# Attention and expert layer on one core: constant rows by DMA, held bulk loads, ordered port turns and a choice among forty orders

## The chip, the core and the metric

The kernel runs on one core of a Trainium2 chip. The core has five engines, each with its own queue of instructions that it works off in order: TensorE (PE in the profile: matrix products, into PSUM), VectorE (DVE), ScalarE (ACT), GpSimd (POOL) and SyncE (SP), which here only issues DMA transfers. Engines wait for one another by semaphores. The metric is the time of one execution on the device, in microseconds (us); smaller is better.

## The reference, cut to what matters

```python
def _attn_ref(q, k, v, s):                 # each 8 x 8 x 576 x 64, s: 8 x 8 x 576
    scores = scale * np.matmul(q, k.transpose(0, 1, 3, 2))
    causal = np.triu(np.ones((S, S), dtype=bool), k=1)
    cum = np.cumsum(np.maximum(s, 0.0), axis=-1)
    bias = -(cum[:, :, :, None] - cum[:, :, None, :])
    scores = np.where(causal, -1000000000.0, scores + np.minimum(bias, 0.0))
    attn = np.exp(scores - np.max(scores, axis=-1, keepdims=True))
    attn = attn / (np.sum(attn, axis=-1, keepdims=True) + 1e-09)
    return np.matmul(attn, v)

def _moe_ref(x, w_gate, w1, w2):           # 4608 tokens of 512, 8 experts of 1024
    flat = (x @ w_gate).flatten()
    for idx in np.argsort(-flat):          # best pair of token and expert first
        tok, e = int(idx) // E, int(idx) % E
        if assigned[tok] >= 0 or counts[e] >= cap:      # cap = 576
            continue
        assigned[tok] = e
        counts[e] += 1
    for e in range(E):
        mask = assigned == e
        out[mask] = np.maximum(x[mask] @ w1[e], 0.0) @ w2[e]
    return out
```

The attention's output, with its 64 (batch, head) planes put side by side as 4608 tokens of 512, is the x of the expert layer.

## The kernel before

**Tiling.** The 64 planes are worked in 16 groups `g` of four (two pairs `pr` of two), so the attention has 32 units, one for each pair. Queries and keys are split into a high and a low 16-bit part, so that products of 16-bit operands keep the precision. `load` (L363) brings a group's q and k into a buffer of the ring `raw` (two buffers), lets ScalarE write the high parts (L409; the first group's also L419) and VectorE the low parts (L411) into a buffer of the ring `QK` (four buffers, QK0 to QK3), and then places copies of these parts at other partitions by DMA, called moves (L416). Rows 64 to 69 of each QK buffer carry constants and, by small DMAs (L397, `auxk`), the cumulated sums. `vload` (L434) does the same for the values (loads L440 into the ring `rv`, high part L442, low part L444 into `Vl`).

**A unit.** First a score pass S (L502, and L486 for its last blocks) puts rough scores into the PSUM ring `pss` (three buffers); VectorE takes row maxima of them (L471, a reduction and a short read of its accumulator each, of 128 to 512 columns); ScalarE and GpSimd split these maxima (L518, L520, L522), TensorE turns them (L524), ScalarE copies them (L526), and a DMA writes them as rows into QK (L529, L530). Then the transposed scores T (L544, L545, L547; at the end L587 to L589) go to the ring `pst`, ScalarE exponentiates them (P, L555), GpSimd forms the rest that P's rounding left (R, L557), and TensorE multiplies P and R with the values (L618 to L620). The output is normalized (L641 to L649), turned (L681) and multiplied with the gate's weights (L692, L693). In the text S0 and T0 are the two passes of the first unit, and so on. Units 0 and 1 use QK0, units 2 and 3 use QK1.

**After the attention** come the routing, a chain of short VectorE steps, and the eight experts, which gather their tokens, turn them and do the two products (L1293, L1297, L1379).

**What sets the order.** No engine's order is written by hand. `Plan` (L88) gets every step as a task with an engine, a duration, dependences, a priority and the ring buffers that it uses, and plays a list schedule: at each point, of the tasks that could start, the one that starts first, by priority among equals. The steps are put on each engine's queue in the order in which this schedule starts them. VectorE and GpSimd share a port to the on-chip memory; tasks that use it are marked `lock`, and the schedule lets such a task start only when the other engine's is over. This is kept in the plan alone: on the chip nothing makes one wait for the other's turn. There are two plans, one for the attention and one for the routing and the experts.

**The start.** `consts` (L248) makes the constants. VectorE fills the constant rows of QK0 and of QK1 (L285, two instructions for each buffer); GpSimd issues two DMAs (L290) that copy QK1's rows to QK2 and QK3, and a gap column of each buffer is zeroed (L297 on GpSimd, L298 on VectorE). The high parts of QK1 wait for its rows and for those two DMAs (`fresh`). Ahead of S0, TensorE does 70 matmuls on zeros (L735, "warm-up"), 55 of which stand ahead of the first score matmul and 15 between score matmuls.

## Time and profile before

| | us |
|---|---|
| time of three runs | 777.54, 777.54, 775.1 (median 777.54) |
| the profiled execution | 777.66 |
| its span in the trace | 775.6 |
| attention / routing / experts in the trace, about | 16 to 310 / 310 to 363 / 363 to 776 |

The profiled execution is 777.66 - 775.6 = 2.06 longer than its span, which is the time around the program. An engine's busy time is the time in which one of its instructions ran; PEld is TensorE's loading of weights, which lies beside its products. In a timeline row, brackets give the idle time of the engine ahead of the instruction and what ended it; rows of one kind next to each other are put together (x55). "TensorE clock" is the share of full speed (2.4 GHz) that was granted: 0.50 is 1.2 GHz. In a tile's name "QK<-QK" is output and input. A DMA's issue stands on the queue of the engine that issues it (SPq, ACTq, POOLq). The rows themselves stand in a section of their own, after the change.

### The profile page before, as it was taken

The page shows a single profiled execution, that of the slowest core. Times are in us where ns is not written, and L with a number is a line of the kernel's source. Part 1 is how long each engine was busy: PE and PEld are TensorE (multiplying, and loading weights), DVE is VectorE, ACT ScalarE, POOL GpSimd, SP SyncE. Part 2 cuts the span into 40 slices and gives each one's busy share as a digit, 9 for nine tenths or more (in the row PEclk, how much of TensorE's full clock was granted, in tenths as well). Part 3 has the DMA queues.
Part 4 walks back from the last instruction along what each step waited for, and adds up shares of the span by engine and source line. Part 5 has one row for each costly group of instructions (what it writes and reads, how often), then busy time and mean ns, then how long its engine had stood idle before and what let it go on. Part 6 is the DMA issues. An engine that isn't in the chain of part 4 may idle for free.

```text
span 775.6 us, 22590 instructions
## 1 busy us (share of the span) xinstructions
PE 722.0 (93%) x8726; PEld 454.9 (59%) x8726; DVE 598.2 (77%) x2014; ACT 391.7 (50%) x794; POOL 335.3 (43%) x428
## 2 busy tenths in 40 slices
PE   9789999999999999628998999999999999999995
PEld 3457788787888888416644544545445454454542
DVE  7889999999999996678895877969788795380110
ACT  3548888888888878405334323324244232461110
POOL 7648988788878988102032041140412224202011
PEclk9679999999999999858999999999999999999998
DMA  7897768686776511106157376394845639851000
GB/s 233 195 213 202 220 175 250 172 241 196 209 203 171 156 35 64 63 35 204 42 167 200 110 113 180 129 222 133 190 156 155 187 105 262 228 180 48 15 28 34
DMA packets 89733, 118.72 MB, mean 153 GB/s; under 512 B 39246, under 2 KB 55758, under 8 KB 89614
## 3 DMA queue, kind: packets, MB, share of 16 engines
q1 hardware_dynamic: 83116, 97.82, 46.1%
q0 software_dynamic: 5952, 19.00, 8.1%
q8 instruction: 68, 1.11, 0.6%
q10 hardware_dynamic: 558, 0.47, 0.2%
q14 instruction: 39, 0.32, 0.1%
HBM read 71.67 MB, written 19.10 MB: 117 GB/s over the span
## 4 chain that ended last, share of the span: by engine, by line
PE 54%; issue 19%; DVE 13%; DMA 5%; POOL 4%; ACT 2%; SPq 1%; POOLq 0%; ACTq 0%; DVEq 0%
PE psm L1293 13%; PE psm L1379 10%; DVE pss L471 5%; PE pst L545 4%; PE pst L544 4%; PE pss L502 3%; PE po L618 3%; PE po L620 2%; PE po L619 2%; POOL out_dram L1352 2%; POOL xg L1226 2%; PE psn L1297 2%; PE po L735 2%; PE pss L681 2%; DMA xg<-xs,ids 1%
## 5 line engine op out<-in xcount | busy, mean ns | idle before, releaser
L557 POOL TENSOR_TENSOR R<-P 128x512 f16<-128x512 f32 (+1 forms) x221 | 218.9, 1016 | 26.9 <-ACT P L555 25.2
L1293 PE MATMUL psm<-xT,w1p 128*128 128x512 f16 (+1 forms) x876 | 193.1, 353 | 1.3 <-DMA xT<-xg 0.8
L1379 PE MATMUL psm<-w2p,hT 128*128 128x512 f16 x768 | 174.4, 379 | 0.0
L555 ACT ACTIVATE P<-pst 128x512 f32<-128x512 f32 (+1 forms) x224 | 119.9, 555 | 25.0 <-PE pst L547 10.3
L1297 PE MATMUL psn<-xT,w1p 128*128 128x64 f16 x768 | 129.7, 193 | 0.0
L471 DVE CUSTOM_DVE_ANT_0 pss<-pss,mS 128x512 f32<-128x512 f32 (+3 forms) x256 | 122.7, 506 | 9.0 <-PE pss L502 8.0
L1293 PEld LDWEIGHTS <-w1p 128*128 128x128 f16 x876 | 79.2, 98 | 80.0 <-issue 1.9
L1352 POOL DMA_INDIRECT out_dram<-y,ids x40 | 39.8, 995 | 198.7 <-ACT y L1390 169.6
L1379 PEld LDWEIGHTS <-hT 128*128 128x128 f16 x768 | 69.0, 98 | 80.3 <-issue 4.4
L1226 POOL DMA_INDIRECT xg<-xs,ids x40 | 43.6, 1089 | 167.3 <-DVE ids L1184 67.3
L618 PE MATMUL po<-V,P 128*128 128x65 f16 x960 | 113.8, 196 | 1.4 <-DVE xp L649 1.0
L620 PE MATMUL po<-V,R 128*128 128x65 f16 x960 | 114.0, 194 | 0.4 <-POOL R L557 0.4
L619 PE MATMUL po<-Vl,P 128*128 128x64 f16 x960 | 113.6, 193 | 0.0
L544 PE MATMUL pst<-QK 70*128 70x64 f16 (+4 forms) x512 | 108.5, 252 | 1.2 <-ACT P L555 0.7
L545 PE MATMUL pst<-QK 128*128 128x64 f16 (+4 forms) x512 | 107.8, 251 | 0.0
L619 PEld LDWEIGHTS <-P 128*128 128x128 bf16 x960 | 90.0, 100 | 9.1 <-issue 2.8
L618 PEld LDWEIGHTS <-P 128*128 128x128 bf16 x960 | 90.4, 98 | 5.9 <-issue 1.8
L1313 ACT ACTIVATE hT<-psm 128x512 f16<-128x512 f32 x64 | 38.2, 597 | 108.1 <-PE psm L1293 88.3
L620 PEld LDWEIGHTS <-R 128*128 128x128 f16 x960 | 89.9, 97 | 0.6 <-POOL R L557 0.6
L1390 ACT ACTIVATE y<-psm 128x512 f32<-128x512 f32 x32 | 19.1, 597 | 122.0 <-PE psm L1379 108.1
L502 PE MATMUL pss<-QK 67*128 67x512 f16 (+3 forms) x256 | 72.6, 307 | 4.7 <-DVE mr L471 2.4
L1297 PEld LDWEIGHTS <-w1p 128*128 128x128 f16 x768 | 67.7, 98 | 1.3
(221 smaller groups left out, 1443.4 us busy)
## 6 DMA issues: line engine op xcount, KB each, us to landing
QK<-QK SPq DMA_DIRECT2D x120, 144.0 KB
wst<-in_w_dram SPq DMA_DIRECT2D x32, 512.0 KB
wst<-in_w_dram SPq DMA_DIRECT2D x64, 256.0 KB
raw<-in_q_dram SPq DMA_DIRECT2D x32, 288.0 KB
raw<-in_k_dram SPq DMA_DIRECT2D x32, 288.0 KB
rv<-in_v_dram SPq DMA_DIRECT2D x32, 288.0 KB
xs<-xp SPq DMA_DIRECT2D x32, 256.0 KB
xs<-xp SPq DMA_DIRECT2D x8, 128.0 KB
```

What stands on the lines that cost most here:

```text
L471: return pl.add("v", dur, lambda: nc.vector.tensor_tensor_reduce(ps(), ps(), mask, 1.0, init() if init else -3e38, OP.add, OP.max, mr.t[:, ...
L502: nc.tensor.matmul(ps.t[:, :n], F()[:, q0:q0 + 128], F()[:, k0:k0 + n], start=True, stop=True)
L544: nc.tensor.matmul(ps[:, c0:c0 + n], F()[:, ks:ks + 128], F()[:, q:q + n], start=True, stop=False)
L545: nc.tensor.matmul(ps[:, c0:c0 + n], G()[:, ks:ks + 128], G()[:, q:q + n], start=False, stop=not diag)
L555: e = pl.add("a", n / 1200 + 0.171, lambda: nc.scalar.activation(P.t[:, c0:c0 + n], ps.t[:, :n], AF.Exp, scale=1.0 / YS), [x] + fresh, pri ...
L557: sub = lambda eng: eng.tensor_tensor(R.t[:, c0:c0 + n], P.t[:, c0:c0 + n], strided_hi(P.t)[:, c0:c0 + n], op=OP.subtract)
L618: nc.tensor.matmul(o[:, i], H[:, c:c + 128], V.t[:, pr, sl], start=f, stop=False)
L619: nc.tensor.matmul(o[:, i, 0:64], H[:, c:c + 128], Vl.t[:, pr, sl], start=False, stop=False)
L620: nc.tensor.matmul(o[:, i], R.t[:, c:c + 128], V.t[:, pr, sl], start=False, stop=l)
L1293: nc.tensor.matmul(ps[:, tiles[0]:tiles[-1] + 1] if len(tiles) > 1 else ps[:, tiles[0]], lhs(f, c, a), xT.t[:, tiles[0]:tiles[-1] + 1, 4 * ...
L1297: nc.tensor.matmul(pt.t[:, 64 * f:64 * f + 64], lhs(f, c, a), xT.t[:, 4, 4 * b + c, 0:64], start=s, stop=e)
L1379: nc.tensor.matmul(py.t, hT.t[:, f, a, 128 * i:128 * i + 128], w2p.t[:, f, b], start=f == 0 and k == 0, stop=f == 7 and k == 2)
```

## The change

1. **Constant rows.** VectorE makes a template `rowc` of 320 columns (two instructions) once. QK0's rows are still filled by VectorE; those of QK1, QK2 and QK3 are written by two DMAs each from the template, issued by GpSimd, QK1's early.
2. **Bulk loads held.** The raw loads of group 2 and the value loads of groups 0 and 1 wait for the first moves (`self.first`: the copies of the high parts) of groups 0 and 1. The high parts of groups 1 and up no longer wait for the constant rows (the passes still do). Moves of group 1 may go on ScalarE's queue too. The router's constants come after QK1's.
3. **Turns at the port.** In the attention's plan each `lock` step of VectorE or GpSimd gets a real dependence on the last such step of the other engine, so that on the chip the turns are taken as in the plan. The plan counts 0.06 for handing over. The experts' plan has no `tc`, and gets none.
4. **Choice of order.** `run` draws 40 orders (all task durations varied by up to 3%; order 0 is without that), replays each four times in its fixed order with random lengthening, and emits the one in which TensorE ends earliest on the mean. A few planned durations change (TensorE's by 1.016, and hops between engines).

```diff
@@ class Plan
+    HAND = 0.06
+    tc = None
+    AFTER = {("t", "a"): 0.05, ("a", "p"): 0.05, ("v", "t"): 0.01}
...
+    ORDERS, SPREAD, DRAWS, NOISE = 40, 0.03, 4, 0.03
+
+    def run(self):
...
+        best = None
+        for n in range(self.ORDERS):
+            reset(n)
+            order = []
+            if not self.order(order.append):
+                continue
+            took = sum(self.replay(order, random.Random(d), clean[0]) for d in range(self.DRAWS)) / self.DRAWS
+            if best is None or took < best[0]:
+                best = took, n
+        reset(best[1])
+        self.order(lambda z: self.emit(*z))
+
+    def replay(self, order, draw, free):
...
+            more = x.occ / x.w * draw.uniform(0.0, self.NOISE)
...
+            if x.lock and e in "vp":
+                t = max(t, port["p" if e == "v" else "v"])
+                port[e] = t + occ + self.HAND
...
+        return max(x.begun for x in self.tasks if x.left == "t")
...
-            return dur, dur + 0.19
+            return dur * 1.016, dur * 1.016 + 0.19
...
+    def emit(self, x, f, e, *_):
+
+        made = f()
+        if x.lock and e in "vp" and self.tc:
+            other = self.held["p" if e == "v" else "v"]
+            if other is not None:
+                self.tc.add_manual_dep(made.ins, other.ins.name, mybir.DependencyInfo(
+                    mybir.DependencyClass.Sync, mybir.DependencyReason.SCHED_ONLY), reason="port")
+            self.held[e] = made
@@ class Attention
+        self.pl.tc = tc
...
+        self.rowc = self.c.tile([128, 2, 320], F16, name="rowc")
+        k["rowc"] = [pl.add("v", 0.2, lambda c=c: nc.vector.tensor_scalar(
+            self.rowc[64:70, c], self.mZ.bitcast(F16)[64:70, 0:320], self.vec[64:70, c:c + 1], None, op0=OP.add),
+            [k["vec", 0, 4], k["vec", 1, 1], k["mZ"]], prio=-93, lock=True) for c in (1, 0)]
...
-            if i < 2:
+            if i < 1:
...
-                made.append(pl.add("p", 0.9, lambda rows=rows: nc.gpsimd.dma_start(rows, self.r["QK"].slots[1][0][64:70, 0]),
-                                   self.rows1 + [k["QK", 1]], prio=-20, kb=62))
-                self.moved.append(made[0])
+                for c in (1, 0):
+                    made.append(pl.add("p", 0.9, lambda rows=rows, c=c: nc.gpsimd.dma_start(
+                        rows[:, c].rearrange("p r (n c) -> p (r n) c", c=320),
+                        self.rowc[64:70, c:c + 1, :].to_broadcast([6, 8, 320])), k["rowc"],
+                        prio=-92 if i == 1 else -20, kb=31))
...
-                          alt=("a", 0.62, lambda: f(nc.scalar.dma_start)) if both and g == 0 else None, **kw)
+                          alt=("a", 0.62, lambda: f(nc.scalar.dma_start)) if both and g < 2 else None, **kw)
...
-                ld[r, t] = Sy(0.5, lambda d, r=r, t=t: d(raw.t[:, t, r], srcs[t][b, :, 2 * hf + r]),
+                ld[r, t] = Sy(0.5, lambda d, r=r, t=t: d(raw.t[:, t, r], srcs[t][b, :, 2 * hf + r]), self.first if g == 2 else [],
...
-        if g == 1:
-            fresh = fresh + self.moved
-
...
-                         [ld[r, t] for r in range(a, z)] + fresh[:1], prio=t0 - 5 + off + t / 10, uses=[raw, QK]) for t in range(2)]
+                         [ld[r, t] for r in range(a, z)] + (fresh[:1] if g == 0 else []), prio=t0 - 5 + off + t / 10,
+                         uses=[raw, QK]) for t in range(2)]
...
+            if a == 0 and g < 2:
+                self.first = e1 + [q2, k2]
...
-        ld = [pl.add("s", 0.45, lambda r=r: nc.sync.dma_start(rv.t[:, r], self.vN[b, :, 2 * hf + r]), prio=t0 - 4.5, uses=[rv],
-                     kb=295, bulk=True) for r in range(2)]
+        ld = [pl.add("s", 0.45, lambda r=r: nc.sync.dma_start(rv.t[:, r], self.vN[b, :, 2 * hf + r]), self.first if g < 2 else [],
+                     prio=t0 - 4.5, uses=[rv], kb=295, bulk=True) for r in range(2)]
...
-        x = None
+        x = self.k["QK", 1]
```

The diff adds lines, so the same step has another number behind it (L285 is L385, L411 is L509, L444 is L544, L471 is L571, L502 is L602).

What the change moves on the engines is seen in three places. The first is SyncE's queue at the start. Before, ahead of QK1's first moves (L416 on QK_92, the last row here; each waits for a high part) stand the loads of group 2 (raw0), of the values (rv) and of the gate's weights (wgf):

```order
L382 DMA raw_87<-in_q_dram 128x576
L416 DMA QK_91<-QK_91 64x576
L382 DMA raw_87<-in_q_dram 128x576
L416 DMA QK_91<-QK_91 64x576
L382 DMA raw_87<-in_k_dram 128x576 x2
L440 DMA rv_90<-in_v_dram 128x576
L327 DMA wgf<-in_w_gate_dram 128x4x8
L440 DMA rv_89<-in_v_dram 128x576
L416 DMA QK_92<-QK_92 64x2x576 x4
```

After (moves L514, raw loads L482, value loads L540, sums L494):

```order
L514 DMA QK_92<-QK_92 64x2x576 x2
L494 DMA QK_92<-auxk 3x2x576 x2
L514 DMA QK_92<-QK_92 64x2x576
L494 DMA QK_93<-auxk 3x2x576
L514 DMA QK_91<-QK_91 64x576
L540 DMA rv_89<-in_v_dram 128x576
L494 DMA QK_93<-auxk 3x2x576
L494 DMA QK_94<-auxk 3x2x576 x2
L482 DMA raw_87<-in_q_dram 128x576 x2
L514 DMA QK_92<-QK_92 64x2x576
L482 DMA raw_87<-in_k_dram 128x576 x2
L540 DMA rv_90<-in_v_dram 128x576 x2
```

QK1's first moves stand ahead of the loads of group 2, three of them on this queue and the fourth on ScalarE's; the k loads of that group (raw0<-in_k_dram) stand behind a QK1 move that waits for VectorE's low parts. Before, those k loads waited for no VectorE step.

The second place is the end of S1 on VectorE and on TensorE. VectorE before, with the value's low part (L444) and then QK1's (L411) between row maxima of the second unit (mr_106; QK_92 is QK1):

```order
L444 SCALAR_TENSOR_TENSOR Vl_98<-rv_89,V_95 128x1152
L471 ISA pss_124,mr_106<-pss_124,mS 128x512
L471 ISA mr_106 128x1
L411 SCALAR_TENSOR_TENSOR QK_92<-raw_88,QK_92 128x2x576 x2
L471 ISA pss_122,mr_106<-pss_122,mS 128x256
```

After:

```order
L509 SCALAR_TENSOR_TENSOR QK_92<-raw_88,QK_92 128x2x576 x2
L571 ISA pss_124,mr_106<-pss_124,mS 128x512
L571 ISA mr_106 128x1
L571 ISA pss_122,mr_106<-pss_122,mS 128x256
L571 ISA mr_106 128x1
L544 SCALAR_TENSOR_TENSOR Vl_98<-rv_89,V_95 128x1152
```

QK1's low parts (L509) went ahead of the maximum over 512 columns, and the value's low part (L544) behind two more maxima. TensorE at the same place, before: the last matmul of S1 (L486) and the start of T0 (L544, L545):

```order
L486 MATMUL pss_124<-QK_91 128x512
L544 LDWEIGHTS QK_91
L544 MATMUL pst_126<-QK_91 128x512
L545 LDWEIGHTS QK_91
L545 MATMUL pst_126<-QK_91 128x512
```

After:

```order
L586 MATMUL pss_124<-QK_91 128x512
L602 LDWEIGHTS QK_92
L602 MATMUL pss_122<-QK_92 128x128
L644 LDWEIGHTS QK_91
L644 MATMUL pst_126<-QK_91 128x512
L645 LDWEIGHTS QK_91
```

The first matmul of the score pass on QK1 (L602 from QK_92) went ahead of T0's first (L644). Ahead of S0's first matmul stand 61 warm-up matmuls in place of 55, and 9 in place of 15 between the score matmuls.

The third place is a turn at the port, some units later, on VectorE (names with their buffer numbers, and what each row waits for). Before:

```order
L471 ISA pss1_123,mr2_107<-pss1_123,mZ_131,mr2_107 128x512 [waits DVE_49,PE_49]
L471 ISA mr2_107 128x1
L444 SCALAR_TENSOR_TENSOR Vl2_100<-rv1_90,V2_97 128x1152 [waits DMAHW1_49,DMAHW0_49]
L645 TENSOR_TENSOR po0_128<-po0_128,den0_114 128x5x64 [waits DVE_49]
L471 ISA pss0_122,mr0_105<-pss0_122,mS_130 128x128 [waits PE_49]
```

After:

```order
L571 ISA pss2_124,mr0_105<-pss2_124,mZ_131,mr0_105 128x512 [waits DVE_49,PE_49]
L571 ISA mr0_105 128x1
L544 SCALAR_TENSOR_TENSOR Vl2_100<-rv1_90,V2_97 128x1152 [waits DMAHW5_49,DMAHW4_49,Pool_49]
L509 SCALAR_TENSOR_TENSOR QK3_94<-raw1_88,QK3_94 128x2x576 [waits DMAHW6_49,DMAHW2_49,DMAHW1_49]
L509 SCALAR_TENSOR_TENSOR QK3_94<-raw1_88,QK3_94 128x2x576 [waits DMAHW7_49,DMAHW5_49,DMAHW1_49]
```

The low part (L544) now waits for GpSimd too (Pool), as the maxima behind it then do by standing behind it. In the attention 15 of the 46 low parts of whole groups (7 of L509, 8 of L544) got such a wait, and some 20 GpSimd steps (11 of R, 9 of the split of the maxima) got one for VectorE; before, no low part waited for GpSimd.

## Rows read from the trace of the kernel before

**Rows 1.** Windows: length, busy us (instructions) of each engine, TensorE clock, DMA share, GB/s.

```profile
16.00:310.00 294.00, 283.48 (x5200) 227.35 (x5198) 277.44 (x912) 234.94 (x540) 231.36 (x261) 0.97 0.66 182
...
363.00:776.00 413.00, 396.60 (x3043) 202.03 (x3039) 269.24 (x917) 133.23 (x215) 81.38 (x115) 0.99 0.50 138
```

**Rows 2.** Windows by the granted clock at the start; columns as above.

```profile
16.00:26.70 10.70, 7.39 (x40) 3.21 (x38) 10.25 (x37) 3.96 (x6) 2.48 (x4) 1.00 0.87 243
26.70:47.20 20.50, 17.63 (x142) 11.80 (x141) 16.95 (x48) 10.42 (x19) 12.66 (x16) 0.50 0.89 191
47.20:57.30 10.10, 8.48 (x135) 5.88 (x133) 8.89 (x30) 5.68 (x15) 5.28 (x10) 1.00 0.96 208
```

**Rows 3.** Windows of the steady attention; columns as above.

```profile
57.30:234.50 177.20, 174.48 (x3353) 143.00 (x3352) 174.10 (x571) 153.08 (x351) 146.28 (x160) 1.00 0.73 208
234.50:293.80 59.30, 59.30 (x1170) 49.03 (x1168) 57.75 (x205) 48.12 (x118) 50.69 (x57) 1.00 0.41 114
```

**Rows 4.** Timeline, TensorE: start, us, line, tiles, shape, count [idle before <-releaser].

```profile
1.61 14.34 PE L735 MATMUL po<-mZ 128*128 128x512 f16 x55 [1.61 <-DVE mZ L258]
...
26.73 0.59 PE L544 MATMUL pst<-QK 70*128 70x512 f16 x1
...
36.08 0.50 PE L502 MATMUL pss<-QK 67*128 67x128 f16 x2 [1.04 <-DMA QK<-auxk]
```

**Rows 5.** Timeline, VectorE; columns as above.

```profile
16.16 0.30 DVE L471 CUSTOM_DVE_ANT_0 pss<-pss,mS 128x128 f32<-128x128 f32 x1 [2.67 <-PE pss L502]
...
21.70 0.88 DVE L285 TENSOR_SCALAR QK<-mZ,vec 6x2560 f16<-6x2560 f16 x1
...
24.23 1.35 DVE L444 SCALAR_TENSOR_TENSOR Vl<-rv,V 128x1152 f16<-128x1152 f32 x1
25.50 0.69 DVE L471 CUSTOM_DVE_ANT_0 pss<-pss,mS 128x512 f32<-128x512 f32 x1
...
26.11 2.62 DVE L411 SCALAR_TENSOR_TENSOR QK<-raw,QK 128x1152 f16<-128x1152 f32 x2
28.65 0.42 DVE L471 CUSTOM_DVE_ANT_0 pss<-pss,mS 128x256 f32<-128x256 f32 x1
...
31.57 0.92 DVE L331 SCALAR_TENSOR_TENSOR wgp<-wgf,wgp 128x32 f16<-128x32 f32 x1
...
36.38 0.30 DVE L471 CUSTOM_DVE_ANT_0 pss<-pss,mS 128x128 f32<-128x128 f32 x1 [2.56 <-PE pss L502]
```

**Rows 6.** Timeline, GpSimd.

```profile
21.46 0.21 POOL L522 TENSOR_TENSOR mp<-ms,mp 128x10 f16<-128x10 f32 x1 [6.14 <-ACT ms L520]
...
23.90 1.32 POOL L290 DMA_DIRECT2D QK<-QK  x2 [0.31 <-POOL QK L297]
```

**Rows 7.** Timeline, ScalarE.

```profile
18.42 1.17 ACT L442 ACTIVATE V<-rv 128x1152 f16<-128x1152 f32 x1 [6.92 <-DMA rv<-in_v_dram]
...
23.40 2.22 ACT L409 ACTIVATE QK<-raw 128x1152 f16<-128x1152 f32 x2 [0.78 <-ACT mt L526]
```

**Rows 8.** Chain that ended last, first 60 us: start, us, what.

```profile
24.37 1.22 DVE Vl L444
...
26.72 6.87 DMA QK<-QK
33.60 2.46 DMA QK<-auxk
```

**Rows 9.** Timeline, SyncE's DMA queue.

```profile
21.27 0.83 SPq L382 DMA_DIRECT2D raw<-in_k_dram  x2
```

**Rows 10.** By form, 16 to 310: count | busy, mean ns | idle before <-releasers.

```profile
L557 POOL TENSOR_TENSOR R<-P 128x512 f16<-128x512 f32 x187 | 202.9, 1108 | 24.9 <-ACT P L555 23.2 <-PE po L693 1.2
...
L411 DVE SCALAR_TENSOR_TENSOR QK<-raw,QK 128x1152 f16<-128x1152 f32 x30 | 42.1, 1410 | 0.0
...
L444 DVE SCALAR_TENSOR_TENSOR Vl<-rv,V 128x1152 f16<-128x1152 f32 x16 | 23.7, 1479 | 0.0
```

**Rows 11.** Waits of TensorE, 363 to 776: total us, times, longest.

```profile
PE psm L1241 <- DMA xg<-xs,ids: 3.7, 3, 1.7
```

82 lines of the change are left out of this document (69 added, 13 removed).

## The prediction

> **What bounds the kernel now.** I read the stages first [rows 1]. In the attention stretch (16 to 310) TensorE is busy 283.48 of 294.00 and VectorE 277.44: both are nearly full, so removing work from one alone gives little there. The routing stretch (310 to 363) is a chain of short VectorE steps; in the experts TensorE is busy 396.60 of 413.00 at a granted clock of 0.99.
>
> Next I cut the attention by clock [rows 2]. From 16 to 26.7 TensorE works only 7.39 of 10.70 while VectorE works 10.25: VectorE's row maxima of the first two score passes (I call a score pass S0, S1, ..., and the transposed scores that follow T0, T1, ...) set the pace. At 26.7 the clock falls to half and stays there for 20.50 us; TensorE is busy 17.63 of them, at double price. From 47.2 to 57.3 the clock is full, and 1.62 (10.10 - 8.48) are idle. After that [rows 3] the two engines run almost without a gap: 174.48 and 174.10 of 177.20. The same kinds of matmul go through at 3353/177.20 = 18.92 per us from 57.3 to 234.5, but at 1170/59.30 = 19.73 from 234.5 to 293.8, where bulk loads are over (DMA share 0.41 against 0.73). At the later pace the long stretch would take 3353/19.73 = 169.9, so the room in it is 7.3 us. That is all that a better order of the steady part could bring.
>
> At the start [rows 4, 5]: 55 warm-up matmuls take 14.34; T0's first matmul starts at 26.73, and the first score pass on the second buffer (QK1) at 36.08, after 1.04 of idle for the DMA that brings its constant and bias rows. VectorE waits 2.67 for the first scores (16.16) and 2.56 for those of QK1 (36.38).
>
> **Constant rows.** Two VectorE fills are gone for QK1: one of 0.88 at 21.70, in the middle of S1's maxima, and one that fell into the idle ahead of 16.16 [rows 5]. The template costs two much shorter VectorE instructions ahead of S0, where VectorE has 2.67 idle: nothing. Instead GpSimd issues six DMAs. An issue like it took 1.32/2 = 0.66 and GpSimd idles 6.14 ahead of 21.46 [rows 6], so six take 3.96 of that, and the transfers are 31 KB each. Covered: 0. A gain of their own they cannot bring, for that is counted at the fill; if the cover were gone, 3.96 would stand ahead of S1's split and of T0.
>
> **The early order.** The high parts of QK1 (ScalarE) no longer wait for the fill. Before, they ran at 23.40 for 2.22, though ScalarE stood idle for 6.92 up to 18.42 [rows 7]. Now they and the first two moves of QK1 can go in that idle, by about 18. A move took 6.87 and the bias rows after it 2.46 [rows 8], so the data of the next score pass are there at about 27.5 instead of 36.08.
>
> T0 itself gets later. There are 61 warm-up matmuls ahead of S0 instead of 55; at 14.34/55 = 0.26 each that is +1.6 [rows 4]. VectorE's chain from the first maximum (16.16) to the point at 24.37 where L444 really begins, without the fill's 0.88, is 7.33. Then, by the new order, come the two low parts of QK1 (2.62), the 512-column maximum (0.69) and the 256-column one (0.42), while L444 falls behind [rows 5, 8]: 16.16 + 1.6 + 7.33 + 2.62 + 0.69 + 0.42 = 28.8. Only then have TensorE's last S1 matmuls and the first of the new pass a free PSUM buffer, and T0 stands behind them. So T0 starts at 28.8, 2.1 late, but the pass on QK1 starts there as well, 7.3 earlier than 36.08.
>
> What comes of it at 57.3, by two ledgers. *TensorE's:* before, half-clock work done by 47.2 was (20.50 - 2.87)/2 = 8.8 us of full-clock work [rows 2]. Now there are 18.4 us from 28.8 to 47.2; the 1.04 wait is gone, the other 1.83 may stay or go: (18.4 - 1.83)/2 = 8.3 to 18.4/2 = 9.2. That is -0.5 to +0.4, taken as 0. From 47.2 to 57.3 I take two thirds of the 1.62 idle as removed, as VectorE then runs ahead: +1.0. *VectorE's:* saved are the fill 0.88, the wait of 2.56, and the 0.92 step at 31.57 that now stands in the idle ahead of S0 [rows 5]; lost is the later start, 1.6: net 2.8. The gain is between 1.0 and 2.8; I take **2.0**, a little nearer the middle than to TensorE's. Ends: -1.5 (the clock comes back 2.1 later too, which costs half of that, and the -0.5) to +2.8.
>
> **Held loads.** The raw loads of the third group and the value loads of the first two now stand behind the first moves. DMA is busy 0.87 to 0.96 of the time up to 57.3 [rows 2], so this shares the same capacity out in another order. One thing is lost: two k loads of the third group, issued at 21.27 [rows 9], now stand on SyncE's queue behind a QK1 move that waits for VectorE's low parts, which end at about 27.7. They come 6.4 late. What is queued behind them is two value loads and more moves; who waits is ScalarE's high part of QK2. I give it 0, since the row maxima of S1 and of QK1's two passes cover it, and keep up to +3 (half of 6.4) for the no-change rival.
>
> **Turns at the port.** In the attention each VectorE or GpSimd instruction that uses the shared port waits for the last such instruction of the other engine in the plan. Behind such a wait on VectorE stand row maxima, for which TensorE waits. What could be gained: the 46 low parts (L411, L444) took 42.1 + 23.7 = 65.8 [rows 10], against 46 x 1.35 = 62.1 at the duration of an undisturbed one [rows 5]: 3.7 stretched by GpSimd. By the order with its waits, 15 of the 46 wait for GpSimd; their stretch turns into a wait of the same length, and the other 31 lose theirs: 31/46 x 3.7 = 2.5. The choice among forty drawn orders has no row of its own; whatever it brings lies within the same 7.3. I take **2.5**, near the stretch that the rows show rather than the whole room, between -5.2 (the last rival) and +7.3.
>
> **The experts.** Their plan has no port waits and is only one of forty near-equal orders; TensorE's queue hardly differs. The largest wait there that an order could touch is 3.7 in 3 times, 1.7 the longest [rows 11]. I take 0, plus or minus 1.7.
>
> **Sum:** 2.0 + 2.5 + 0 = 4.5. The profiled execution took 777.66 (span 775.6), 0.12 above the median 777.54, so it may stand for it: 777.66 - 4.5 = **773.2**.
>
> **Rivals.**
> *The clock.* The half-clock stretch begins when TensorE has waited through S1, and lasts 20.50 us although TensorE is busy 17.63 of them [rows 2]. The new order closes the 1.04 wait and puts score and transposed work side by side; the clock might come back after a quarter of the stretch or not fall at all. The whole stretch costs 17.63/2 = 8.8, half of it 4.4; the middle, 6.6, gives 766.6. Against it: up to 28.8 TensorE waits as much as before or more. The Trainium skill (TensorE: Matmul & The Clock Gate, "What's actually happening") says that the throttled state is the default and that activity releases it; by that rule closer work would bring the clock back sooner, and these rows, 20.50 us at half with TensorE 86% busy, do not bear it out well.
>
> *It does not do what it says.* The pass on QK1 comes 7 us earlier, but VectorE still has to do the same maxima, and the k loads of the third group come later; the early gain is spent by 57.3, and the steady part, with both engines at 98%, goes on at 18.92 per us. That gives 777.7, or with the 3 of the late loads 780 at most.
>
> *The row DMAs are held by VectorE.* If each of the six issues must wait for one VectorE instruction like the low parts (2.62/2 = 1.31), they take 6 x (0.66 + 1.31) = 11.8, which is 5.7 more than the idle 6.14: 773.2 + 5.7 = 778.9. Against it: the two issues from 23.90 ran beside L444 in 1.32 [rows 5, 6]. The Trainium skill (SBUF — State Buffer, "SBUF: two separate sides") warns of this: a DMA issued by GpSimd needs descriptors that GpSimd cannot write while VectorE holds the shared port. It speaks against this change; the row just named does not show it.
>
> *Slower: waits for a turn.* A fixed order makes VectorE wait for GpSimd's residual (L557, 1.108 mean [rows 10]) even when GpSimd is late, where before the first to come went first. If the 15 low parts that wait for GpSimd each stand half of one, 0.55, VectorE loses 8.3. Its slack from 57.3 to 234.5 is 177.20 - 174.10 = 3.1 [rows 3], so 5.2 reach TensorE: 777.66 - 2.0 + 5.2 = 780.9. It decides from a mean wait of (3.1 + 2.0)/15 = 0.34 on (no gain left); at 0.50 it is slower by 0.3%. For it: VectorE has no other room. Against: GpSimd is idle 24.9 in L557's rows alone, most of it waiting for ScalarE [rows 10], so it is seldom late by a whole instruction.
>
> **How the numbers follow.** About 0.3%, 2.3 us, is what a measurement of this kernel can tell from no change: faster is below 775.2, slower above 779.9. Forecast (769 to 775.2) 0.45; clock back early 0.10; nothing changed 0.21; row DMAs held 0.04; waits for a turn 0.20. Faster 0.45 + 0.10 = 0.55, same 0.21 + 0.04 = 0.25, slower 0.20. The range reaches from 765.5 (the clock rival less 1.1 for the uncertain steady part) to 781.5 (the slower rival and 0.6); left out are half of the slower rival's spread and a little of the clock's, under 2 in 10.
>
> **What would show it.** Right: no 0.88 fill ahead of T0, T0 at about 28.8, the first score matmul of QK1 at about 28.5 instead of 36.08; a half-clock stretch of about 20 us; L411's and L444's means near 1.36; some 19.2 matmuls per us in the long stretch. Wrong: row DMAs of over 1.5 each; VectorE idle for GpSimd's L557 (over 5 us in all); TensorE waiting for QK2's moves between 40 and 57; an experts stretch that changes by more than 2 us.

## The result, and the profile after

The changed kernel takes 785.41 us (median of 4, 783.52 to 786.9) against 777.54 for the kernel before, 7.87 more. The ratio on record is 1.0123, with a 95% interval of 1.01 to 1.0145; the quotient of the two medians is 1.0101, which lies inside it. It is **slower by 1.0 to 1.2%**, where 773.2 was forecast and 781.5 was the upper end. The profiled execution, the slowest of the four, took 786.9, with a span of 785.2 (before 775.6).

To see where it went, both traces are cut where TensorE has done the same number of matmuls (warm-ups left out). The table gives the time at which a mark is reached.

| mark | before | after | difference |
|---|---|---|---|
| first score matmul (S0) | 15.79 | 22.07 | +6.3 |
| first transposed score (T0) | 26.73 | 35.87 | +9.1 |
| start of the long stretch of 4427 matmuls | 67.7 | 70.0 | +2.3 |
| its end | 296.4 | 304.7 | +8.3 |
| first product of the experts (L1293, then L1394) | 361.0 | 370.2 | +9.2 |
| end of the span | 775.6 | 785.2 | +9.6 |

So 8.3 of the 9.6 are lost ahead of the routing and 0.9 between there and the experts, which take about as long as before. Two things stand out: a start that is 6 to 9 us late, and a stretch of the same number of matmuls that takes 6 us longer. In between, TensorE catches up much of the first.

The start. Windows of the changed kernel by the granted clock (columns as in [rows 2], which answer to it):

```profile
16.00:21.20 5.20, 1.87 (x9) 0.67 (x7) 1.47 (x4) 1.26 (x2) 1.25 (x5) 1.00 0.39 43
21.20:28.00 6.80, 5.93 (x19) 2.56 (x20) 4.09 (x17) 2.22 (x2) 4.12 (x14) 0.50 0.84 211
28.00:31.70 3.70, 2.20 (x13) 1.01 (x12) 3.21 (x17) 0.58 (x3) 0.79 (x3) 0.96 0.53 135
31.70:51.90 20.20, 17.43 (x161) 12.19 (x161) 15.55 (x46) 9.29 (x18) 6.95 (x10) 0.50 0.70 201
51.90:60.00 8.10, 7.97 (x94) 5.37 (x92) 7.63 (x29) 7.24 (x16) 6.28 (x8) 1.00 0.71 190
```

There are two half-clock stretches, 6.80 and 20.20 long, where before had one of 20.50. GpSimd's timeline at the start, then VectorE's, then TensorE's, then three pieces of the chain that ended last:

```profile
3.14 0.12 POOL L370 MEMSET vec<- 32x1 f32 x2 [2.61 <-DVE V L354]
...
6.21 0.53 POOL L357 TENSOR_SCALAR_AFFINE_SELECT mU<-mU 64x64 bf16<-64x64 bf16 x2
11.92 3.66 POOL L391 DMA_DIRECT2D QK<-rowc  x6 [5.18 <-DVE rowc L376]
```

```profile
6.78 0.88 DVE L385 TENSOR_SCALAR QK<-mZ,vec 6x2560 f16<-6x2560 f16 x1 [3.69 <-POOL mU L357]
...
8.17 0.88 DVE L385 TENSOR_SCALAR QK<-mZ,vec 6x2560 f16<-6x2560 f16 x1
9.07 1.35 DVE L450 TENSOR_TENSOR_SCAN xp<-xp,mZ 64x576 f32<-64x576 f32 x1
...
22.48 0.43 DVE L571 CUSTOM_DVE_ANT_0 pss<-pss,mS 128x256 f32<-128x256 f32 x1 [3.24 <-PE pss L602]
...
31.62 2.62 DVE L509 SCALAR_TENSOR_TENSOR QK<-raw,QK 128x1152 f16<-128x1152 f32 x2
```

```profile
1.62 16.26 PE L835 MATMUL po<-mZ 128*128 128x512 f16 x61 [1.62 <-DVE mZ L354]
22.07 0.80 PE L602 MATMUL pss<-QK 67*128 67x256 f16 x3 [4.20 <-issue]
...
34.96 1.01 PE L586 MATMUL pss<-QK 67*128 67x512 f16 x2 [2.56 <-DVE mr L571]
35.77 0.31 PE L602 MATMUL pss<-QK 67*128 67x128 f16 x1
35.87 0.63 PE L644 MATMUL pst<-QK 70*128 70x512 f16 x1
```

```profile
13.64 0.45 DVE QK L509
14.09 6.88 DMA QK<-xp
20.97 1.10 issue
```

GpSimd's first constant waits 2.61 for VectorE's memsets (3.14), and VectorE's first fill of QK0's rows then waits 3.69 for GpSimd's masks (6.78): turns at the port among the constants, where a fill reads nothing of the masks that it waits for. The scan that starts the cumulated sums runs at 9.07; before it ran at 5.50. The sums' row for S0 leaves at 14.09, takes 6.88 and lets S0 start at 22.07, after 4.20 of idle (the row says "issue", the chain shows the transfer). Then L385 is gone from S1 and the low parts of QK1 stand at 31.62, as the order said; T0 follows S1's end at 35.87, and QK1's pass starts at 35.77, no earlier than before [rows 4].

The long stretch, before and then after (windows; both have about 4427 matmuls, though not quite the same ones: after has 0.3% more columns, by estimate 0.8 us of the 6.0):

```profile
67.70:296.40 228.70, 226.26 (x4428) 186.68 (x4425) 223.60 (x748) 194.34 (x454) 190.85 (x210) 1.00 0.64 181
```

```profile
70.00:304.70 234.70, 230.91 (x4427) 188.25 (x4425) 224.35 (x744) 194.25 (x455) 170.14 (x209) 1.00 0.65 183
```

VectorE is as busy as before (223.60 and 224.35) but the stretch is 6.0 longer. After's rows by form that answer to [rows 10], over this stretch, and VectorE's waits in it (total, times, longest), before and after:

```profile
L657 POOL TENSOR_TENSOR R<-P 128x512 f16<-128x512 f32 x156 | 157.8, 1040 | 25.3 <-ACT P L655 15.5 <-DVE Vl L544 5.0 <-DVE QK L509 4.7
...
L509 DVE SCALAR_TENSOR_TENSOR QK<-raw,QK 128x1152 f16<-128x1152 f32 x26 | 34.2, 1351 | 0.0
...
L544 DVE SCALAR_TENSOR_TENSOR Vl<-rv,V 128x1152 f16<-128x1152 f32 x14 | 18.9, 1353 | 0.1
```

```profile
DVE pss L471 <- PE pss L502: 1.3, 5, 0.5
```

```profile
DVE pss L571 <- PE pss L602: 3.2, 10, 0.5
DVE pss L571 <- PE pss L586: 1.3, 6, 0.3
```

The low parts run at 1.35 and the residuals at 1.04: the stretching by the port is gone altogether, as intended. In return VectorE waits more often for scores (the listed waits 1.3 before, 3.2 + 1.3 after), and GpSimd waits for VectorE's low parts (5.0 + 4.7).

### The profile page after: what moved, and what is told of

The parts are those of the page before. It is cut to its first block, busy times and chain, and to the rows that moved or that the text cites. A ratio compares the mean times of both kernels' runs of the same rounds, so it can differ in the third digit from the quotient of the medians.

```text
span 785.2 us, 22607 instructions
## 1 busy us (share of the span) xinstructions
PE 730.8 (93%) x8726; PEld 458.1 (58%) x8726; DVE 590.5 (75%) x2018; ACT 389.8 (50%) x793; POOL 311.4 (40%) x429
## 4 chain that ended last, share of the span: by engine, by line
PE 55%; issue 19%; DVE 15%; POOL 6%; DMA 3%; ACT 1%; POOLq 0%; SPq 0%; DVEq 0%; ACTq 0%
PE psm L1394 12%; PE psm L1480 11%; DVE pss L571 4%; PE pst L644 4%; PE pst L645 4%; PE pss L602 3%; PE po L718 3%; PE po L720 2%; PE po L719 2%; POOL out_dram L1453 2%; POOL R L657 2%; DVE QK L509 2%; PE psn L1398 2%; PE pss L781 2%; PE pss L586 2%
## 5 line engine op out<-in xcount | busy, mean ns | idle before, releaser
L657 POOL TENSOR_TENSOR R<-P 128x512 f16<-128x512 f32 (+1 forms) x223 | 204.1, 948 | 38.9 <-ACT P L655 22.5
L1394 PE MATMUL psm<-xT,w1p 128*128 128x512 f16 (+1 forms) x876 | 194.0, 353 | 1.2 <-ACT xT L1344 1.1
L571 DVE CUSTOM_DVE_ANT_0 pss<-pss,mS 128x512 f32<-128x512 f32 (+3 forms) x256 | 123.3, 505 | 12.5 <-PE pss L602 11.0
L1453 POOL DMA_INDIRECT out_dram<-y,ids x40 | 41.5, 1038 | 218.6 <-ACT y L1491 189.3
L655 ACT ACTIVATE P<-pst 128x512 f32<-128x512 f32 (+1 forms) x224 | 118.0, 554 | 20.5 <-PE pst L647 9.3
L1394 PEld LDWEIGHTS <-w1p 128*128 128x128 f16 x876 | 79.4, 98 | 80.6 <-issue 2.6
L644 PE MATMUL pst<-QK 70*128 70x64 f16 (+4 forms) x512 | 105.9, 250 | 0.1
L645 PE MATMUL pst<-QK 128*128 128x64 f16 (+4 forms) x512 | 105.4, 250 | 0.0
L602 PE MATMUL pss<-QK 67*128 67x512 f16 (+3 forms) x256 | 74.4, 313 | 6.8 <-issue 4.2
L1416 DVE SCALAR_TENSOR_TENSOR hT<-psm,hT 128x512 f16<-128x512 f32 x64 | 43.9, 686 | 39.5 <-ACT hT L1414 37.9
```

The costliest lines, as they stand in the source:

```text
L571: return pl.add("v", dur, lambda: nc.vector.tensor_tensor_reduce(ps(), ps(), mask, 1.0, init() if init else -3e38, OP.add, OP.max, mr.t[:, ...
L602: nc.tensor.matmul(ps.t[:, :n], F()[:, q0:q0 + 128], F()[:, k0:k0 + n], start=True, stop=True)
L644: nc.tensor.matmul(ps[:, c0:c0 + n], F()[:, ks:ks + 128], F()[:, q:q + n], start=True, stop=False)
L645: nc.tensor.matmul(ps[:, c0:c0 + n], G()[:, ks:ks + 128], G()[:, q:q + n], start=False, stop=not diag)
L655: e = pl.add("a", n / 1200 + 0.171, lambda: nc.scalar.activation(P.t[:, c0:c0 + n], ps.t[:, :n], AF.Exp, scale=1.0 / YS), [x] + fresh, pri ...
L657: sub = lambda eng: eng.tensor_tensor(R.t[:, c0:c0 + n], P.t[:, c0:c0 + n], strided_hi(P.t)[:, c0:c0 + n], op=OP.subtract)
```

## The experiments

Each group of runs has its own runs of the kernel before, so the ratio is what counts (as on record; the quotient of the medians differs from it by up to 0.3%). "Stretch" is the time that the long stretch takes in one trace (before 228.7, after 234.7). Runs are numbered by group; the expectations say "call" for a group.

| run | rows by DMA | held loads | waits for turns | hand-over | orders | ratio to before (95%) | stretch |
|---|---|---|---|---|---|---|---|
| changed kernel | yes | yes | all | 0.06 | 40 | 1.0123 (1.0100 to 1.0145) | 234.7 |
| 1.1 | yes | yes | none | 0.06 | 40 | 1.0153 (1.0096 to 1.0210) | 246.1 |
| 1.2 | yes | yes | all | 0 | 40 | 1.0126 (1.0077 to 1.0175) | 237.6 |
| 1.3 | yes | yes | after constants | 0.06 | 40 | 1.0038 (1.0010 to 1.0065) | 235.8 |
| 1.4 | yes | yes | all | 0.06 | 1 | 1.0114 (1.0080 to 1.0147) | 233.0 |
| 2.1 | yes | yes | none | 0 | 1 | 1.0105 (1.0085 to 1.0124) | 238.1 |
| 2.2 | yes | yes | after constants | 0 | 1 | 1.0108 (1.0084 to 1.0133) | 241.4 |
| 2.3 | no | no | after constants | 0 | 1 | 1.0038 (1.0019 to 1.0057) | 232.4 |
| 2.4 | yes | yes | none | 0 | 40 | 1.0061 (1.0038 to 1.0083) | 240.5 |
| 3.1 | no | no | none | 0 | 1 | 0.9985 (0.9958 to 1.0013) | 228.7 |
| 3.2 | yes | yes | after constants | 0.06 | 40 | 0.9992 (0.9977 to 1.0007) | 234.7 |
| 3.3 | yes | yes | after constants | 0.06 | 40 | 1.0064 (1.0043 to 1.0086) | 233.3 |
| 3.4 | no | yes | after constants | 0.06 | 40 | 1.0015 (1.0002 to 1.0027) | 232.5 |
| 4.1 | yes | no | none | 0 | 1 | 1.0135 (1.0108 to 1.0163) | 240.1 |
| 4.2 | no | yes | none | 0 | 1 | 1.0068 (1.0050 to 1.0085) | 239.7 |
| 4.3 | no | no | after constants | 0.06 | 1 | 1.0045 (1.0024 to 1.0066) | 237.2 |
| 4.4 | no | yes | after constants | 0.06 | 40 | 0.9979 (0.9965 to 0.9993) | 232.6 |
| 5.1 | yes | yes | constants only | 0.06 | 40 | 1.0227 (1.0202 to 1.0251) | 246.9 |
| 5.2 | no | no | all | 0 | 1 | 1.0153 (1.0123 to 1.0182) | 232.8 |

The columns tell of the attention's plan. The experts are planned by forty orders in all of them, with the numbers of before (no hand-over, no 1.016, no extra hops) in 2.1 to 2.4, 3.1, 3.2, 4.1 to 4.4 and 5.2 (in 4.3 with the hand-over), with the changed ones elsewhere (in 1.2 the hand-over is 0 there too). This shows in the ratios: from the first product of the experts to the end the traces take 414.6 before, 412.8 to 415.7 with the changed numbers, and 409.4 to 412.6 in all eleven runs with those of before. So the ratios of these eleven hold some 2 to 5 us that aren't the attention's. Runs 3.3 and 3.4 are described below.

**Group 1: which part of the change.** Run 1.1 takes the added waits out and leaves the order:

```diff
-        self.pl.tc = tc
```

> The changed kernel, same instruction order on every engine, without the added waits between VectorE and GpSimd. Theory O (the order that the plan made costs the time: low parts stand three in a row on VectorE, 4.05 us; the waits cost only at the start): first score matmul at about 17.9 instead of 22.07, first transposed score at about 30 instead of 35.87, from 70 to 300 us the same pace as the changed kernel (about 6 us slower than before), L657 stretched again; time 783 (781 to 784.5). Rival W (the waits cost the time): the whole loss goes, time 777 (775 to 779).

Run 1.2 sets the hand-over in the plan to 0:

```diff
-    HAND = 0.06
+    HAND = 0.0
```

> The changed kernel with the hand-over of 0.06 in the plan set to 0 and nothing else; waits between the engines stay. All 46 low parts then stand alone on VectorE. Theory O: the pace from 70 to 300 us is that of before again, so 6 us of the loss go; the start still has waits among the constants; time 779.5 (777 to 782). Rival W: more changes of turn and so more waits, 785 or more.

Run 1.3 keeps the waits, but not for the steps of the constants (with which the sums, the gate's weights and the router's constants count here):

```diff
-            if other is not None:
+            if other is not None and x.rank >= self.steady:
...
         self.k["router"] = x
+        pl.steady = pl.n
```

> The changed kernel, same order, with the added waits only for steps after the constants. Theory O: the steady waits cost nothing that shows, so this is within 1.5 us of the run without any waits: 783 (781 to 785), first score matmul at about 17.9. Rival W: the steady waits cost 6, so 783 here against 777 there.

Run 1.4 takes the first drawing:

```diff
         self.pl.tc = tc
+        self.pl.ORDERS = 1
```

> The changed kernel with the attention's order taken from the first, undisturbed drawing instead of the best of forty. Theory O: the bunches of three are there as well (11 of them against 10), so the time is that of the changed kernel within 2 us: 785 (783 to 787). Rival: the replay chooses an order that is bad on the chip, and the first drawing gives 780 or less.

Measured: 789.36, 786.58, 778.61 and 785.18, where before gave 775.25. On 1.1 and 1.3 both theories fell; 1.2 came as W had it (785 or more) and 1.4 as O had it. Without any waits the kernel is not better but, if anything, worse (1.0153); with the waits after the constants alone it loses only 0.4%. So the waits are two things: those after the constants are worth about 9 us *in this order* (1.1 against 1.3, whose intervals leave 4 to 14), and those among the constants cost about 7 (1.3 against the changed kernel). VectorE and then TensorE at the start of 1.3:

```profile
3.12 0.92 DVE L385 TENSOR_SCALAR QK<-mZ,vec 6x2560 f16<-6x2560 f16 x1
...
4.65 1.00 DVE L385 TENSOR_SCALAR QK<-mZ,vec 6x2560 f16<-6x2560 f16 x1
5.69 1.35 DVE L450 TENSOR_TENSOR_SCAN xp<-xp,mZ 64x576 f32<-64x576 f32 x1
```

```profile
1.62 15.74 PE L836 MATMUL po<-mZ 128*128 128x512 f16 x61 [1.62 <-DVE mZ L354]
18.71 0.51 PE L602 MATMUL pss<-QK 67*128 67x256 f16 x3 [1.35 <-issue]
...
30.06 0.63 PE L644 MATMUL pst<-QK 70*128 70x512 f16 x1
```

The fills stand at 3.12 and 4.65 instead of 6.78 and 8.17, S0 at 18.71 instead of 22.07, T0 at 30.06 instead of 35.87. The clock goes with it: in 1.3 it stands at 0.50 for 6.80 us ahead of the long stretch, where the changed kernel has 6.80 and 20.20 and the kernel before 20.50:

```profile
27.00:33.80 6.80, 4.65 (x25) 2.64 (x25) 5.42 (x13) 2.87 (x4) 1.86 (x2) 0.50 0.93 221
```

One trace could be chance, but every execution has its mean granted clock on record. As these traces show only the two levels 0.50 and 1.00, 2 x (1 - clock) x span is an estimate of an execution's time at half clock. On the mean that is 64 us in the changed kernel (clock 0.9592, four executions), 52 in 1.3 (0.9662, ten) and 60 in the kernel before (0.9614, 79). In the long stretch, the windows of 1.1 and of 1.3, and 1.1's rows by form:

```profile
61.30:307.40 246.10, 234.58 (x4428) 189.40 (x4425) 234.78 (x745) 195.38 (x455) 207.04 (x210) 1.00 0.62 175
```

```profile
60.70:296.50 235.80, 231.21 (x4428) 188.34 (x4425) 224.49 (x745) 194.22 (x455) 170.44 (x209) 1.00 0.65 182
```

```profile
L656 POOL TENSOR_TENSOR R<-P 128x512 f16<-128x512 f32 x157 | 179.0, 1165 | 15.3 <-ACT P L654 13.7 <-ACT den L740 0.8 <-PE po L719 0.2
...
L508 DVE SCALAR_TENSOR_TENSOR QK<-raw,QK 128x1152 f16<-128x1152 f32 x26 | 38.9, 1530 | 0.0
...
L543 DVE SCALAR_TENSOR_TENSOR Vl<-rv,V 128x1152 f16<-128x1152 f32 x14 | 22.2, 1586 | 0.0
```

Without the waits this order sets VectorE and GpSimd against each other: low parts of 1.53 and 1.59, residuals of 1.17, and 246.1 for the stretch. With them 235.8. Neither comes to 228.7.

The hand-over (1.2) was expected to give 6 us back, as the low parts then stand singly (46 alone; with it, 10 triples). It gave nothing: VectorE then waits for GpSimd's residuals, which in the changed kernel's long stretch it hardly did:

```profile
DVE QK L509 <- POOL R L657: 3.2, 12, 0.4
DVE Vl L544 <- POOL R L657: 2.7, 8, 0.6
```

The choice among forty (1.4) changes nothing that can be told apart (785.18 against 785.41).

**Group 2: the parts without the new plan numbers.** Run 2.1 is the first two parts alone; 2.2 adds the waits after the constants, 2.3 puts these waits on the kernel before's own order, 2.4 is 2.1 with forty orders. 2.1's edit of the changed kernel:

```diff
-    HAND = 0.06
+    HAND = 0.0
...
-    AFTER = {("t", "a"): 0.05, ("a", "p"): 0.05, ("v", "t"): 0.01}
+    AFTER = {}
...
-            return dur * 1.016, dur * 1.016 + 0.19
+            return dur, dur + 0.19
...
-        self.pl.tc = tc
+        self.pl.ORDERS = 1
```

> Parts 1 and 2 of the change alone (constant rows by DMA, held loads) in the attention: no added waits, hand-over 0, the planned durations of before, one order instead of forty. Theory P (the first two parts gain 6 to 8 us at the start; the steady loss of 6 to 7 belongs to the turns and to the plan's numbers): a lead of about 6 at 65 us that is kept, time 770 (767 to 773). Rival Q (the lead cannot be kept in any order, since both engines are full): 776 (774 to 779).

2.2 (and 2.3, which has the kernel before's `consts`, `load` and `vload` as well) adds to that the lines of 1.3 and:

```diff
+        self.pl.tc = tc
```

> As the first run of this call, with the added waits for all steps after the constants. Without the hand-over in the plan the low parts stand alone and VectorE changes turn with GpSimd often. Theory P: VectorE waits some 7 us for L657, and the kernel is 5 us slower than the run without waits: 775 (772 to 778). Rival R (keeping the planned turns is worth about 10 in any order, as it was in the changed kernel's order): 5 or more faster than the run without.

> The attention of the kernel before, instruction for instruction, with the added waits for all steps after the constants and nothing else. Theory P: the waits replace a stretch of 3.7 by waits of 5 to 8 on VectorE: 779 (777 to 782), against 775 of before here. Rival R: 770 or less.

2.4 leaves out `self.pl.ORDERS = 1`.

> As the first run of this call, but the best of forty orders by the replay. Theory P: no difference beyond 2 us to the run with one order, since the replay does not know what stretches on the chip: 770 (767 to 774). Rival: the replay picks an order that is better by 4 or more, 766 or less.

Measured: 782.08, 782.49, 776.22 and 778.71; before 773.42. The lead at the start is there in 2.4 (5.3 us at 67.7, with T0 at 28.71, where 28.8 was forecast for the changed kernel) and small in 2.1 (1.7, T0 at 33.84), but both lose 9 to 12 in the long stretch. Waits on the order of before (2.3) cost 3.8 there, of the expected kind. Its window and VectorE's waits:

```profile
66.30:298.80 232.50, 229.77 (x4428) 188.22 (x4424) 221.91 (x748) 196.49 (x454) 172.09 (x211) 1.00 0.63 178
```

```profile
DVE QK L508 <- POOL R L655: 3.6, 14, 0.5
DVE Vl L542 <- POOL R L655: 1.2, 5, 0.3
```

VectorE now waits 3.6 + 1.2 for residuals. So of theory P, the waits' cost holds for before's order (2.3 against 3.1, which has the same attention without waits: 1.0038 and 0.9985). It isn't seen in the whole time of 2.2 against 2.1 (1.0108 and 1.0105), where P had 5 us and rival R as much the other way. That the first two parts gain 6 to 8, and keep it, fell, and so did rival Q's 776. Forty orders gave 3.4 (2.1 against 2.4), a little more than expected.

**Group 3: the experts, and what delays S0.** 3.1 has before's attention and only the experts planned anew; 3.2 is 1.3 with the experts planned by the numbers of before:

```diff
-    HAND = 0.06
+    HAND = 0.0
...
-    AFTER = {("t", "a"): 0.05, ("a", "p"): 0.05, ("v", "t"): 0.01}
+    MUL = 1.0
+    AFTER = {}
...
-            return dur * 1.016, dur * 1.016 + 0.19
+            return dur * self.MUL, dur * self.MUL + 0.19
...
         self.pl.tc = tc
+        self.pl.HAND, self.pl.MUL = 0.06, 1.016
+        self.pl.AFTER = {("t", "a"): 0.05, ("a", "p"): 0.05, ("v", "t"): 0.01}
```

> The attention of the kernel before, instruction for instruction, and of the change only the choice among forty orders for the routing and the experts, planned with the numbers of before (no hand-over, no factor 1.016, no extra hops). Theory E (in the runs with these numbers the experts ended 3.5 to 5.6 us earlier against the attention than before, while with the changed numbers they gained 0 to 1.4): time 4 less than before, 770 (768 to 772) where before gives 774. Rival: the gain came from what the attention left over at its end, and the time is that of before.

> The changed kernel with the added waits only after the constants (the third run of the first call, same attention order), and the routing and experts planned with the numbers of before. Theory E: 3 to 4 us less than that run, so about 1 us below before: 773 (771 to 776). Rival: no change against that run, 777.

3.3 is 1.3 with the gate's weights loaded later; 3.4 is 1.3 with `consts` filling the rows as before:

```diff
-        ld = pl.add("s", 0.35, lambda: nc.sync.dma_start(self.wgf, self.wg.rearrange("(c p) e -> p c e", p=128)), prio=-1,
+        ld = pl.add("s", 0.35, lambda: nc.sync.dma_start(self.wgf, self.wg.rearrange("(c p) e -> p c e", p=128)), [self.k["auxk"]], prio=-1,
```

> As the third run of the first call, but the load of the gate's weights (16 KB in many small packets, there issued at 5.61 ahead of the sums' rows) waits for the sums' last transfer. Theory F (that load holds up the small DMAs of the sums' rows, of which one took 6.90): first score matmul right behind the 59 warm-ups, at about 17.5 instead of 18.71, rows under 4 us. Rival G (the six row DMAs of GpSimd hold them up): first score matmul at 18.7 or later. The steady order is drawn anew, so the whole time is open within 6 us: 777 (772 to 784).

> As the third run of the first call, but with the constant rows made as before (two VectorE fills for QK1, two copies for QK2 and QK3). Theory F: the sums' rows are as late as there, the first score matmul at 18.7 or later (63 warm-ups, 18.3 at the earliest). Rival G: it follows the warm-ups at 18.3, and the rows land in under 4 us. The fills cost VectorE 0.88 in the second unit. Whole time open within 6 us: 778 (772 to 784).

Measured: 774.33, 776.18, 781.88 and 777.65; before 776.51. The experts' gain in the traces (2.7 us in 3.1, 3.7 in 3.2, from the first product to the end) shows as 0.9985 and, against 1.3, 0.9992 after 1.0038; neither can be told from the kernel before. On S0: moving the load of the gate's weights (3.3) left 1.69 and 0.66 of idle ahead of the first two groups of scores (the first ends with a high part of ScalarE, the second with a row of the sums), while with the old rows (3.4) S0 follows the warm-ups at once, though the load of the weights is early there too (5.5). So theory G held and F fell:

```profile
1.61 16.06 PE L832 MATMUL po<-mZ 128*128 128x512 f16 x63 [1.61 <-DVE mZ L354]
17.51 0.49 PE L598 MATMUL pss<-QK 67*128 67x256 f16 x3
```

**Group 4: rows, holds, bunches, and a better version.** 4.1 is 2.1 with before's `load` and `vload`, 4.2 is 2.1 with before's rows; no line is new. 4.3 is 2.3 with the hand-over:

```diff
-    HAND = 0.0
+    HAND = 0.06
```

> Attention with part 1 alone (constant rows by DMA from the template), no added waits, the numbers of before, one order; experts as in the last two calls. Theory G (the six row DMAs hold up the sums' rows): over 1.3 us of idle between the warm-ups and the first score matmul, as in the run with parts 1 and 2. Theory S (without waits every newly drawn order loses in the steady part, since it sets low parts and residuals against each other): from the same point of TensorE's work at about 68 to that at about 296 it takes 234 to 241 instead of 228.6; time 781 (777 to 785). Rival: only one of the two parts disturbs the steady order, and this one gives 774 to 777.

> Attention with part 2 alone (loads held behind the first moves, the high parts of the second group not waiting for the constant rows), otherwise as the run above. Theory G: no idle between the warm-ups and the first score matmul. Theory S: the steady part takes 234 to 241; time 780 (776 to 784). Rival: 772 to 775, if the loss of both parts together is that of the rows.

> Attention of the kernel before with the hand-over of 0.06 in the plan and the added waits after the constants; neither the rows nor the holds nor forty orders. The low parts then stand in bunches, as in the changed kernel. Theory B (a bunch of three makes VectorE wait for scores afterwards): VectorE waits 5 or more us for score matmuls in the steady part instead of 2.0, which takes 233 to 236 instead of 228.6. Rival (the bunches are harmless, the rows and holds disturb the order): 229 to 231.

4.4 joins 3.4 with the lines of 3.2.

> The version to which the runs point: held loads, waits only after the constants, forty orders, constant rows as before, and the experts planned with the numbers of before. Its attention is that of the fourth run of the last call, 0.5 us ahead of before at its end; the experts bring 3 to 4: 773 (771 to 775) where before gives 776.5. Rival: the experts' gain isn't there in the whole time, 776 to 777.5.

Measured: 784.28, 778.97, 775.85 and 771.63; before 773.84. TensorE at the start of 4.1 and of 4.2:

```profile
1.61 14.42 PE L834 MATMUL po<-mZ 128*128 128x512 f16 x57 [1.61 <-DVE mZ L354]
19.15 0.92 PE L601 MATMUL pss<-QK 67*128 67x128 f16 x3 [3.12 <-DMA auxk<-xp]
```

```profile
1.61 13.22 PE L831 MATMUL po<-mZ 128*128 128x512 f16 x53 [1.61 <-DVE mZ L354]
14.66 0.49 PE L598 MATMUL pss<-QK 67*128 67x256 f16 x3
```

4.1 idles 3.12 ahead of S0, 4.2 not at all. Over all runs this is clean: each run with row DMAs by GpSimd has between 1.32 and 6.93 of idle there, and each without has none, but for 5.2, where the constants wait for turns. (Between 52 and 68 warm-ups stand ahead of S0, so the size of this idle can't be compared.) SyncE's queue shows where the time goes. Run 2.1 differs from 4.2 by the way the rows are made alone, and first 2.1, then 4.2 have:

```profile
11.54 3.95 SPq L427 DMA_DIRECT2D wgf<-in_w_gate_dram  x1
```

```profile
11.55 0.65 SPq L423 DMA_DIRECT2D wgf<-in_w_gate_dram  x1
```

In both the same rows of the sums and `auxk` stand next on this queue, so in 2.1 they are 3.3 us later, and S0 starts at 18.52 instead of 14.66. In the long stretch both parts lose alike (240.1 and 239.7): it is not one of them alone that disturbs the order; each new order that was run without waits behind the constants (1.1 and 5.1, which share one, 2.1, 2.4, 4.1, 4.2) takes 238 to 247. Bunches (4.3): the stretch and VectorE's waits for scores:

```profile
61.50:298.80 237.30, 230.06 (x4427) 187.25 (x4425) 227.26 (x743) 193.45 (x455) 171.10 (x209) 1.00 0.66 179
```

```profile
DVE pss L569 <- PE pss L600: 3.7, 11, 0.6
DVE pss L569 <- PE pss L584: 1.3, 7, 0.3
```

The expected 5 us of waits for scores are there (3.7 + 1.3), and the stretch is 237.2, above the forecast.

4.4 takes 771.63 against 773.84, 0.9979 (0.9965 to 0.9993): it beats both kernels, the one before by 0.2%, half of what was expected. In its trace, 5.9 us shorter than before's, 4.5 of these lie in the experts (410.1 against 414.6), so this is no proof of a gain in the attention.

**Group 5: the waits among the constants alone.** 5.1 is 1.3 with the condition turned round, 5.2 is 2.3 with all waits.

```diff
-            if other is not None and x.rank >= self.steady:
+            if other is not None and x.rank < self.steady:
```

> The changed kernel, same order, with the added waits only among the constants and none after them: the fourth corner beside the changed kernel (both), the run without any waits, and the one with the waits after the constants. Theory C (the waits among the constants cost 6 to 8 by a first score matmul 3 to 4 us later and a half-clock stretch more, whatever the rest does): first score matmul at about 22, time 7 above the run without waits, 1.024 of before, that is about 794 (790 to 798). Rival: the loss at the start is given back in the steady part, and the time is that of the run without waits, 1.015 of before.

> Attention of the kernel before with all added waits, among the constants too; against the run of before's attention with the waits after the constants only (1.0038 of before). Theory C: the first score matmul comes 3 to 7 us later than its 16, and the time is 1.010 to 1.013 of before: 782 to 784. Rival: with before's order of the constants the waits cost nothing, 1.004.

Measured: 793.4 (1.0227) and 787.94 (1.0153); before 775.82. TensorE at the start of 5.1:

```profile
1.61 15.19 PE L836 MATMUL po<-mZ 128*128 128x512 f16 x61 [1.61 <-DVE mZ L354]
21.99 0.80 PE L602 MATMUL pss<-QK 67*128 67x256 f16 x3 [5.19 <-DMA QK<-xp]
```

With 1.1, 1.3 and the changed kernel, this is a square in one and the same order: no waits 1.0153, among the constants 1.0227, after them 1.0038, both 1.0123. The waits among the constants cost 0.74% (5.7 us) alone and 0.85% (6.6) beside the others; the waits after them bring 1.0 to 1.2%. In the order of before, the waits among the constants cost 1.0153 - 1.0038, 1.15% or 8.9 us (7.7 in the traces up to the end of the long stretch). By the intervals the 6.6 and the 8.9 are uncertain by 2.8 either way, the 5.7 by 4.8. Part of the price is clock: by the estimate above the time at half clock is longer by 4 us (5.1 against 1.1), 11 (changed kernel against 1.3) and 12 (5.2 against 2.3), which at double price makes up to 1.9, 5.7 and 6.1 us.

## Why the prediction was wrong, step by step

**Both terms of the sum failed.** By the marks, 2.0 were to be gained at the start and 2.3 were lost there; 2.5 were to be gained in the long stretch and 6.0 were lost.

**Constant rows: half right.** The fill is gone, and the six issues took 3.66 (0.61 each; 0.66 was taken) in GpSimd's idle time. "Covered: 0" was wrong all the same: what they hold up is not an engine but the sums' rows, on which S0 waits. Of these one took 6.88, and idle of 1.32 to 6.93 stands ahead of S0 in every run with row DMAs. The traces show two forms of it: an issue on SyncE's queue that takes long (3.95 against 0.65 in the pair above), and a row of the sums that takes 4.2 to 7.0 from issue to landing (1.2, 1.4, 3.3, 4.1, 5.1 and the changed kernel), where in 5.2, without row DMAs, S0 starts 2.2 after the last such issue. What in the chip makes them long no run shows. The held-descriptor warning of the Trainium skill (SBUF — State Buffer, "SBUF: two separate sides") isn't seen: the issues took 0.56 to 0.83 each, several of them while VectorE's low parts ran.

**The early order: the sum was right, its start was not.** From the first maximum on, VectorE's chain and T0 came as worked out: in 1.3, S0 at 18.71 gives T0 at 30.06, 11.4 later; the forecast had 11.4 from 17.4 to 28.8. In the changed kernel S0 stood at 22.07, and T0 came 13.8 behind it, 2.4 more than forecast, with the half-clock stretch of 6.80 between them.

**Turns at the port: the step that failed.** It costed the waits of 15 low parts and no others. The text itself says that *each* such instruction waits, but the constants ahead of S0 (memsets, masks, fills) are such instructions too, they are on the path to S0, and a wait like the fill's of 3.69 for the masks serves nothing that the fill reads. The prediction put that at nothing, without a reason. Their price is 5.7 to 8.9 us in three pairs of runs, beside a loss of the changed kernel of 7.9 (medians) to 9.6 (ratio and traces); without them 0.4% is left. The chain begins with GpSimd's first `vec` memset, which waits for VectorE (3.14).

**The steady gain: the other step that failed, right about the low parts' stretch, wrong about its worth.** The low parts went to 1.35 as forecast, but the 2.5 us were to come from an order that stays as good as before's. A new order that keeps turns cheap (hand-over 0.06) bunches the low parts by three, 4.05 us, and VectorE then waits for scores; one that doesn't waits for residuals. All of these are 4 to 13 us slower in the long stretch than before's order without waits. The lead of 7.0 at 67.7 in run 1.3 was spent there, as the no-change rival had it (whose upper figure is 777.7 + 3 = 780.7, not 780). Why before's own order does so well untouched is not shown by any of these runs; it is the only one of those without waits that stays under 235. So the cause of the 6.0 stays open in part.

**The slower rival** had the right sign (780.9, 3.2 more than before, where 7.9 were measured) by another mechanism: VectorE hardly waited for L657 in the changed kernel's long stretch; GpSimd waited for VectorE. Its mechanism is seen in 1.2 and 2.3 (5.9 and 4.8 us).

**The clock rival** fell for the changed kernel: the second half-clock stretch is 20.20 long with TensorE at 86% busy, like before's, and the late start added one of 6.80, in which 5.93 us of work were done at double price: 3.0 us. But it is much of what 1.3 shows, the same order without the waits among the constants. There 6.80 stood at half clock instead of 20.50, so up to (20.50 - 6.80)/2 = 6.9 of its lead of 7.0 may be the clock's, and not the early order's, which was forecast to bring 2.0 at an unchanged clock. Over all executions it is less: some 7 us fewer at half clock than in the kernel before, so under 4 us of time.

**The experts** came as forecast: 414.6 before, 415.0 after. What the forecast didn't see is that the choice among forty orders does bring something there, 2 to 5 us in the traces, when the plan keeps the numbers of before.
